# Scaling the exponentials of a banded attention by their inverse sums before they are transposed

## The chip, the cores and the metric

The kernel runs on one core of a Trainium2 chip. The metric is the device time of one execution in microseconds. Three runs of the kernel before took 2136.72, 2136.96 and 2138.09 us, a median of 2136.96 us.

The engines have these names in the profile: PE is TensorE (matrix products and transposes), DVE is VectorE, ACT is ScalarE, POOL is GpSimd, SP issues the DMAs. Each runs its own queue in order, and semaphores join the queues.

## The reference

A banded attention feeds a mixture of experts. Only the attention is touched by the change:

```python
scores = scale * np.matmul(q, k.transpose(0, 1, 3, 2))
...
scores = np.where(keep, scores, -1000000000.0)
scores = scores - np.max(scores, axis=-1, keepdims=True)
a = np.exp(scores)
a = a / (np.sum(a, axis=-1, keepdims=True) + 1e-09)
return np.matmul(a, v).astype(np.float32)
```

The sizes are 4 batches, 8 heads, 768 positions and a head width of 64. A query sees the first 8 keys and the 96 keys that end with itself. All is float32. Behind it, 3072 rows of width 512 go through a gate, eight Sinkhorn steps on the gate's weights, and 8 experts with a hidden width of 1024.

## The kernel before, in words

The attention is cut into 32 pieces of work: batch, half of the sequence, and pair of heads. A piece n has three tiles of 128 queries (UT = 3), and a group is one tile of queries for both heads of the pair, so there are 96 groups t = 3n + group. Because the mask is a band, a tile of queries meets at most two blocks of 128 keys, and a group holds two score blocks of 128x256 (128x128 at the very start of a sequence). Groups are handled in chunks of two (CHUNK = 2), so the attention stage is 48 chunks.

For one chunk the steps are these, and one chunk's score steps run two chunks ahead of its transposes (AHEAD = 4 groups):

- `prepare` (L251 on): TensorE transposes the queries and keys of a later piece; ScalarE copies the result rounded (L266), VectorE subtracts to get the remainder (L267), and GpSimd copies key blocks (L275 to L282). The next load of q and k is issued behind it.
- `scores`: TensorE multiplies into two PSUM banks, one for each head of the pair, both groups side by side. There is only one buffer for each bank, so the next chunk's products wait until VectorE has read this one's.
- `softmax` (L335, L339): VectorE adds the bias, writes the block to `p_sb` in SBUF and gets the row's extreme in `mx`; ScalarE takes the exponential in place and sums each row into `sm`.
- After the last group of a piece (L342 to L345) VectorE adds EPS to the six columns of `sm` and takes the reciprocal; ScalarE spreads the result over 64 columns for each head, into `inv`, 128x384.
- `turn`: TensorE transposes the exponentials, ScalarE copies them to `pT`.
- `place`, `flush`: when the piece ends, `invert` has TensorE transpose `inv` (three 128x128 blocks, `r_ps`) and VectorE copy it back (L450). TensorE multiplies the transposed exponentials with the values into `o_ps`. VectorE multiplies `o_ps` by `inv` (L436), ScalarE copies it rounded to `xh` (L439), and VectorE subtracts to get `xl` (L441). `flush` also issues the load of the values of piece n + 2.

So the outputs come out transposed, the queries along the columns, and the inverse sums have to be turned and spread before they can be multiplied with them.

Beside the attention, in the same stage and in the gaps that `between` gives it, run parts of the expert layer: hidden layers of the first expert on TensorE, the gate, and sums of the attention's outputs (`combine`, L684 to L694) on GpSimd, 128x512 each. DMAs are issued by SP alone.

TensorE's order in the attention is that of the program. The other engines' orders are set by a scheduler when the kernel is built.

Of the kernel before, what the change touches and what calls it, by code (L numbers as in the profile page):

```python
# [8 lines left out]
F32 = mybir.dt.float32  # L9
# [3 lines left out]
ALU = mybir.AluOpType  # L13
# [4 lines left out]
P = 128  # L18
# [4 lines left out]
EPS = 1e-9  # L23
UT = 3
# [23 lines left out]
GROUPS = (((0, 0), (1, 0)), ((0, 1), (1, 1)), ((0, 2), (1, 2)))  # L48
# [44 lines left out]
class InOrder:  # L93


    def __init__(self, tc):
        self.tc, self.engine = tc, tc.nc.tensor
# [8 lines left out]
class Banded:  # L106
# [6 lines left out]
    def __init__(self, tc, q, k, v, early):  # L113

        self.tc, self.nc = tc, tc.nc
        self.q, self.k, self.v = q, k, v
        self.H, self.D = q.shape[1], q.shape[3]
        H, nb = self.H, 3 * self.H * P
        self.bias1 = early[:, 0:2 * H * P].rearrange("p (h c) -> p h c", h=H)
        self.bias0 = early[:, 2 * H * P:nb].rearrange("p (h c) -> p h c", h=H)  # L120
        self.early_raw = early[:, nb:nb + self.RAW]
        nb += self.RAW
        self.d1 = early[:, nb:nb + 2 * P]
        self.d0 = early[:, nb + 2 * P:nb + 3 * P]
        self.work = [(b, half, g) for b in range(q.shape[0]) for half in range(2) for g in range(H // 2)]
        self.pending = []
        self.sums, self.inv, self.outs = {}, {}, {}
        self.pe = InOrder(tc)
        nb += 3 * P
        self.early_pT = early[:, nb:nb + 4 * P].rearrange("p (c k) -> p c k", c=4)  # L130
        assert nb + 4 * P <= early.shape[1] - 256
        self.warm = early[:, -256:].bitcast(mybir.dt.bfloat16)
        self.qk, self.vs, self.ready, self.scored, self.far, self.copied, self.loaded = {}, {}, {}, {}, {}, {}, {}
# [182 lines left out]
    def softmax(self, t, s_list):  # L316


        nc, D = self.nc, self.D
        n, group = divmod(t, len(GROUPS))  # L320
        _, half, g = self.work[n]
        blocks = self.key_blocks(half)[1]
        p_sb = self.wrk.tile([P, 2, 2, P], F32, name="p_sb")
        mx = self.wrk.tile([P, 2], F32, name="mx", bufs=4)
        if group == 0:
            self.sums[n] = self.wrk.tile([P, UT, 2], F32, name="sm", bufs=4)
        sm = self.sums[n]
        views = []
        for u, (j, i) in enumerate(GROUPS[group]):
            h = 2 * g + j  # L330
            nb = len(blocks[i])
            bias = self.bias0[:, h] if nb == 1 else self.bias1[:, h]
            pv = p_sb[:, u, 0:nb].rearrange("p a c -> p (a c)")
            views.append(pv)
            nc.vector.tensor_tensor_reduce(out=pv, in0=s_list[u], in1=bias, scale=-(D ** -0.5), scalar=3.0e38,  # L335
                                           op0=ALU.add, op1=ALU.min, accum_out=mx[:, u:u + 1])
        for u, pv in enumerate(views):
            j, i = GROUPS[group][u]
            nc.scalar.activation(out=pv, in_=pv, func=AF.Exp, bias=mx[:, u:u + 1], scale=-1.0,  # L339
                                 accum_out=sm[:, i, j:j + 1])  # L340
        if group == len(GROUPS) - 1:
            nc.vector.tensor_scalar(out=sm, in0=sm, scalar1=EPS, scalar2=None, op0=ALU.add)  # L342
            nc.vector.reciprocal(out=sm, in_=sm)
            self.inv[n] = self.wrk.tile([P, UT, P], F32, name="inv", bufs=3)
            nc.scalar.copy(out=self.inv[n].rearrange("p t (j d) -> p (t j) d", j=2),  # L345
                           in_=sm.rearrange("p t j -> p (t j)").unsqueeze(2).broadcast_to([P, 2 * UT, D]))
        return p_sb

    def blocks(self, n, group):
# [63 lines left out]
    def place(self, turned, x):  # L413

        for t, pT in turned:
            n, group = divmod(t, len(GROUPS))
            if group == len(GROUPS) - 1:
                self.invert(n)
            if group == 0:
                self.outs[n] = self.ps.tile([P, UT, P], F32, name="o_ps", tag="o", bufs=2)  # L420
            self.pending.append((n, group, pT, self.outs[n], n % (self.H // 2), x))

    def flush(self):


        ended = None
        for n, group, pT, o_ps, g, x in self.pending:
            self.values(n, group, pT, o_ps)
            if group == len(GROUPS) - 1:
                ended = n, o_ps, g, x  # L430
        self.pending = []
        if ended is None:
            return
        n, o_ps, g, x = ended
        self.load_v(n + 2)
        self.nc.vector.tensor_tensor(out=o_ps, in0=o_ps, in1=self.inv.pop(n), op=ALU.mult)  # L436
        of = o_ps.rearrange("p t c -> p (t c)")
        for xh, xl, src, dst, width in x:
            self.nc.scalar.copy(out=xh[:, g, dst:dst + width], in_=of[:, src:src + width])  # L439
        for xh, xl, src, dst, width in x:  # L440
            self.nc.vector.tensor_tensor(out=xl[:, g, dst:dst + width], in0=of[:, src:src + width],  # L441
                                         in1=xh[:, g, dst:dst + width], op=ALU.subtract)

    def invert(self, n):

        inv = self.inv[n]
        r_ps = self.ps.tile([P, 4, P], F32, name="r_ps", tag="tp") if self.idle else self.turned("r_ps")
        for i in range(UT):
            self.pe.transpose(out=r_ps[:, i], in_=inv[:, i], identity=self.ident)
        self.nc.vector.tensor_copy(inv, r_ps[:, 0:UT])  # L450


class Dense:
# [938 lines left out]
```

## Time and profile before

The profiled execution took 2136.92 us, and its span from the first to the last instruction is 2135.1 us.

| what | before |
|---|---|
| median of three runs | 2136.96 us |
| profiled execution | 2136.92 us |
| its span | 2135.1 us |
| mean granted TensorE clock | 0.999 |
| first and last start of the score operation (L335) | 12.2 and 262.6 us |
| last start of L441, the remainder of an output | 276.7 us |
| TensorE busy, 400 to 1000 us | 600.0 of 600 us |

The attention stage is about the first 277 us. What follows is the expert layer. A row of groups gives the line, the engine, the operation, output and inputs by their names in the program, the shapes and the count; then the busy time in us and the mean of one instruction in ns; then the time that the engine sat idle just ahead of it, with what ended it. A row of a line's or a tile's instructions gives the shortest, the median and the longest in ns, and the first and last start in us. A row of the timeline gives the start and the duration in us.

### The profile page before, as it was taken

How to read it: one execution, taken by the hardware profiler on the slowest of the kernel's cores; microseconds unless marked ns; L12 is line 12 of the kernel's file. 1: busy time of each engine (PE TensorE's matmuls, PEld its weight loads, DVE VectorE, ACT ScalarE, POOL GpSimd, SP SyncE). 2: the span in 40 equal slices, each digit the busy share in tenths (PEclk: the TensorE clock that was granted, in tenths of full speed). 3: DMA queues.
4: the chain of work that ended last, by engine and by line, in shares of the span. 5: the costliest groups of instructions: out<-in, count | busy, mean ns of one | idle time of the engine just before them, and what ended most of it. 6: DMA issues, size and time to landing. Idle time of an engine off the chain costs nothing.

```text
span 2135.1 us, 31170 instructions
## 1 busy us (share of the span) xinstructions
PE 2107.4 (99%) x10440; PEld 1729.6 (81%) x10441; DVE 1492.1 (70%) x2278; ACT 744.8 (35%) x1539; POOL 1513.6 (71%) x1361
## 2 busy tenths in 40 slices
PE   9999999999999999999999999999999999999998
PEld 6877768888888888888888888888788888888886
DVE  7666678655555565557777777777667777777776
ACT  7778743333332333323222222222242222222221
POOL 5685887777777777537777777777767777777775
PEclk9999999999999999999999999999999999999999
DMA  6687555756657566597777777777976777677662
GB/s 157 156 215 184 141 201 218 266 220 244 232 212 265 210 234 238 203 395 224 202 195 204 203 195 203 203 196 202 340 242 194 203 203 199 199 203 203 194 194 82
DMA packets 294872, 452.40 MB, mean 212 GB/s; under 512 B 114160, under 2 KB 153264, under 8 KB 284336
## 3 DMA queue, kind: packets, MB, share of 16 engines
q1 hardware_dynamic: 294704, 450.31, 67.5%
q8 instruction: 87, 1.43, 0.3%
q14 instruction: 81, 0.66, 0.1%
HBM read 310.92 MB, written 139.30 MB: 211 GB/s over the span
## 4 chain that ended last, share of the span: by engine, by line
PE 94%; DVE 3%; ACT 2%; POOL 1%; issue 0%; DMA 0%; SPq 0%; DVEq 0%; POOLq 0%; ACTq 0%
PE m_ps L100 27%; PE y_ps L100 16%; PE bank_x L100 11%; PE bank_z L100 11%; PE bank_w L100 11%; PE bank_y L100 6%; PE s_ps L100 2%; PE o_ps L100 2%; PE t_ps L103 1%; PE h_ps L100 1%; ACT p_sb L339 1%; PE tp L103 1%; PE y_ps L774 1%; PE y_ps L775 1%; PE y_ps L776 1%; DVE sm L342 0%
## 5 line engine op out<-in xcount | busy, mean ns | idle before, releaser
L100 PE MATMUL m_ps<-hop,w2r 128*128 128x512 f32 x2520 | 639.5, 389 | 1.4 <-DVE m L1298 1.4
L1298 DVE TENSOR_TENSOR m<-m_ps,m 128x1024 f32<-128x1024 f32 x406 | 495.3, 1220 | 194.6 <-PE m_ps L100 191.4
L100 PEld LDWEIGHTS m_ps<-hop,w2r 128*128 128x128 f32 x2520 | 472.9, 188 | 100.2 <-DVE m L1298 1.8
L872 POOL TENSOR_TENSOR hop<-h,hop 128x512 fp32r<-128x512 f32 x180 | 233.1, 1295 | 303.4 <-ACT hop L871 303.4
L100 PE MATMUL y_ps<-w2ops,hop 128*128 128x512 f32 x1344 | 336.8, 389 | 0.0
L872 POOL TENSOR_TENSOR hop<-hsum,hop 128x512 fp32r<-128x512 f32 x240 | 305.1, 1292 | 0.9 <-ACT hop L871 0.9
L871 ACT CAST hop<-hsum 128x512 fp32r<-128x512 f32 x240 | 149.5, 623 | 426.6 <-POOL hsum L877 423.0
L100 PEld LDWEIGHTS y_ps<-w2ops,hop 128*128 128x128 f32 x1344 | 252.3, 188 | 52.3
L1145 DVE SCALAR_TENSOR_TENSOR acc<-y_ps,pm,acc 128x512 f32<-128x512 f32 x240 | 179.8, 750 | 143.1 <-PE y_ps L100 141.9
L871 ACT CAST hop<-h 128x512 fp32r<-128x512 f32 x180 | 111.8, 621 | 379.2 <-DVE h L883 373.8
L100 PE MATMUL bank_z<-xr,w1r 128*128 128x512 f32 x744 | 189.0, 389 | 0.0
L100 PE MATMUL bank_w<-xr,w1r 128*128 128x512 f32 x744 | 189.0, 389 | 0.0
L100 PE MATMUL bank_x<-xr,w1r 128*128 128x512 f32 x744 | 188.9, 389 | 0.0
L877 POOL TENSOR_TENSOR hsum<-h,h 128x512 f32<-128x512 f32 x120 | 153.1, 1297 | 41.1 <-DVE h L883 41.0
L100 PEld LDWEIGHTS bank_x<-xr,w1r 128*128 128x128 f32 x744 | 139.6, 188 | 28.9
L100 PEld LDWEIGHTS bank_z<-xr,w1r 128*128 128x128 f32 x744 | 139.5, 188 | 28.8
L100 PEld LDWEIGHTS bank_w<-xr,w1r 128*128 128x128 f32 x744 | 139.5, 188 | 28.8
L877 POOL TENSOR_TENSOR hsum<-h,hsum 128x512 f32<-128x512 f32 x120 | 155.4, 1295 | 0.0
L339 ACT ACTIVATE p_sb<-p_sb,mx 128x256 f32<-128x256 f32 (+1 forms) x192 | 93.0, 493 | 34.9 <-DVE mx L335 34.9
L615 POOL TENSOR_TENSOR wsum<-w1f 128x256 f32<-128x256 f32 x62 | 44.9, 746 | 84.7 <-DMA w1f<-in_moe_w_dram 84.7
L100 PE MATMUL bank_y<-xr,w1r 128*128 128x512 f32 x372 | 94.4, 389 | 0.0
L748 DVE TENSOR_TENSOR t<-bank_y,t 128x512 f32<-128x512 f32 x93 | 64.2, 690 | 39.2 <-PE bank_y L100 38.2
(263 smaller groups left out, 3383.9 us busy)
## 6 DMA issues: line engine op xcount, KB each, us to landing
w1r<-w1s SPq DMA_DIRECT2D x434, 256.0 KB, 3.0
w2r<-w2s SPq DMA_DIRECT2D x420, 256.0 KB, 3.0
w1s<-w1ops SPq DMA_DIRECT2D x31, 1792.0 KB, 6.8
w2s<-s2ops SPq DMA_DIRECT2D x30, 1024.0 KB, 8.4
w2s<-w2ops SPq DMA_DIRECT2D x30, 768.0 KB, 7.7
w1f<-in_moe_w_dram SPq DMA_DIRECT2D x32, 512.0 KB, 7.8
w2f<-in_moe_w_dram SPq DMA_DIRECT2D x32, 512.0 KB, 8.6
xs_t<-piece SPq DMA_DIRECT2D x16, 512.0 KB, 3.5
```

The costliest lines, as they stand in the source:

```text
L100: return self.tc.keep_in_program_order(self.engine.matmul(*args, **kw))
L103: return self.tc.keep_in_program_order(self.engine.transpose(*args, **kw))
L339: nc.scalar.activation(out=pv, in_=pv, func=AF.Exp, bias=mx[:, u:u + 1], scale=-1.0, accum_out=sm[:, i, j:j + 1])
L615: self.nc.gpsimd.tensor_tensor(out=s[:, n], in0=x, in1=y, op=op)
L748: tt(out=t, in0=bank["y"], in1=t, op=ALU.add)
L774: self.pe.matmul(y_ps, lhsT=hh, rhs=lf, start=(f == 0), stop=False, skip_group_check=True)
L775: self.pe.matmul(y_ps, lhsT=hl, rhs=wf, start=False, stop=False, skip_group_check=True)
L871: self.nc.scalar.copy(out=t[:, 0], in_=full)
L872: self.nc.gpsimd.tensor_tensor(out=t[:, 1], in0=full, in1=t[:, 0], op=ALU.subtract)
L877: self.nc.gpsimd.tensor_tensor(out=t, in0=self.full[x], in1=self.full[y], op=ALU.subtract)
L1145: nc.vector.scalar_tensor_tensor(out=a, in0=y_ps, scalar=moe.pm[:, tt, e:e + 1], in1=a, op0=ALU.mult, op1=ALU.add)
L1298: nc.vector.tensor_tensor(out=ms[p], in0=bank, in1=ms[p], op=ALU.add)
```

## The change

Each group's sums are made ready on their own, the exponentials are multiplied with the inverse sums in SBUF, ahead of their transposes, and everything that turned and applied the inverse sums later is taken out.

```diff
-        if group == 0:
-            self.sums[n] = self.wrk.tile([P, UT, 2], F32, name="sm", bufs=4)
-        sm = self.sums[n]
+        sm = self.wrk.tile([P, 2], F32, name="sm", bufs=4)
...
         for u, pv in enumerate(views):
-            j, i = GROUPS[group][u]
             nc.scalar.activation(out=pv, in_=pv, func=AF.Exp, bias=mx[:, u:u + 1], scale=-1.0,
-                                 accum_out=sm[:, i, j:j + 1])
-        if group == len(GROUPS) - 1:
-            nc.vector.tensor_scalar(out=sm, in0=sm, scalar1=EPS, scalar2=None, op0=ALU.add)
-            nc.vector.reciprocal(out=sm, in_=sm)
-            self.inv[n] = self.wrk.tile([P, UT, P], F32, name="inv", bufs=3)
-            nc.scalar.copy(out=self.inv[n].rearrange("p t (j d) -> p (t j) d", j=2),
-                           in_=sm.rearrange("p t j -> p (t j)").unsqueeze(2).broadcast_to([P, 2 * UT, D]))
+                                 accum_out=sm[:, u:u + 1])
+        nc.vector.tensor_scalar(out=sm, in0=sm, scalar1=EPS, scalar2=None, op0=ALU.add)
+        nc.vector.reciprocal(out=sm, in_=sm)
+        for u, pv in enumerate(views):
+            nc.vector.tensor_scalar(out=pv, in0=pv, scalar1=sm[:, u:u + 1], scalar2=None, op0=ALU.mult)
         return p_sb
...
-            if group == len(GROUPS) - 1:
-                self.invert(n)
...
-        self.nc.vector.tensor_tensor(out=o_ps, in0=o_ps, in1=self.inv.pop(n), op=ALU.mult)
...
-    def invert(self, n):
-
-        inv = self.inv[n]
-        r_ps = self.ps.tile([P, 4, P], F32, name="r_ps", tag="tp") if self.idle else self.turned("r_ps")
-        for i in range(UT):
-            self.pe.transpose(out=r_ps[:, i], in_=inv[:, i], identity=self.ident)
-        self.nc.vector.tensor_copy(inv, r_ps[:, 0:UT])
```

Where the scheduler puts the new instructions is seen in VectorE's queue. Before, this stands between the score operations of the 29th and the 30th chunk (the number behind a score buffer tells the buffers apart; ISA is the score operation, L335):

```order
L342 TENSOR_SCALAR sm<-sm 128x6
L343 RECIPROCAL sm<-sm 128x6
L267 TENSOR_TENSOR qq<-tp,qq 128x384
L436 TENSOR_TENSOR o_ps<-o_ps,inv 128x384
L267 TENSOR_TENSOR kk<-tp,kk 128x3x128
L441 TENSOR_TENSOR xl<-o_ps,xh 128x384
L335 ISA p_sb,mx<-s_ps_2861,acc 128x256
```

Now, at the same place, where the line numbers are those of the changed kernel (L338 was L342, L333 was L335, L433 was L441, and L341 is the new multiplication):

```order
L338 TENSOR_SCALAR sm<-sm 128x2
L339 RECIPROCAL sm<-sm 128x2
L338 TENSOR_SCALAR sm<-sm 128x2
L341 TENSOR_SCALAR p_sb<-p_sb,sm 128x256 x2
L339 RECIPROCAL sm<-sm 128x2
L267 TENSOR_TENSOR qq<-tp,qq 128x384
L267 TENSOR_TENSOR kk<-tp,kk 128x3x128
L341 TENSOR_SCALAR p_sb<-p_sb,sm 128x128 x2
L433 TENSOR_TENSOR xl<-o_ps,xh 128x384
L333 ISA p_sb,mx<-s_ps_2947,acc 128x256
```

The product with the outputs is gone, and both groups of the chunk now have their addition, their reciprocal and their two multiplications between one chunk's score operations and the next one's; the remainders of q and k stand behind the first group's multiplications.

On TensorE, this stood just ahead of the next chunk's score products before:

```order
L100 MATMUL o_ps<-acc 64x128 x2
L100 MATMUL o_ps<-pT,acc 64x128 x4
L103 MATMUL t_ps<-ident,p_sb 128x128 x6
L103 MATMUL r_ps<-ident,inv 128x128 x3
L100 MATMUL s_ps_2936<-kk,qq 128x256
```

Now the same place reads:

```order
L100 MATMUL o_ps<-acc 64x128 x2
L100 MATMUL o_ps<-pT,acc 64x128 x4
L103 MATMUL t_ps<-ident,p_sb 128x128 x6
L100 MATMUL s_ps_3023<-kk,qq 128x256
```

The three transposes of the inverse sums are gone, and nothing else of TensorE's order has moved there.

More of the change, by code (lines that the diff above doesn't have):

```diff
@@ L126, in __init__ @@
         self.pending = []
-        self.sums, self.inv, self.outs = {}, {}, {}
+        self.outs = {}
         self.pe = InOrder(tc)
```

## The prediction

> **What bounds the kernel now.** The page's first part and the shares of the chain that ended last come first.
>
> ```profile
> PE 2107.4 (99%) x10440; PEld 1729.6 (81%) x10441; DVE 1492.1 (70%) x2278; ACT 744.8 (35%) x1539; POOL 1513.6 (71%) x1361
> ...
> PE 94%; DVE 3%; ACT 2%; POOL 1%; issue 0%; DMA 0%; SPq 0%; DVEq 0%; POOLq 0%; ACTq 0%
> ```
>
> TensorE is busy 99% of the span and holds 94% of the chain, so taking work from TensorE should pay and giving work to VectorE (70%) should not matter. Those are averages over the whole span. The change touches the attention stage alone, so the table by windows comes next, cut at 277 us, where the last attention output is split.
>
> ```profile
> core 0: us, PE busy (x) PEld busy (x) DVE busy (x) ACT busy (x) POOL busy (x), PEclk, DMA share, GB/s
> 0.00:277.00 277.00, 263.67 (x2290) 206.21 (x2291) 184.26 (x661) 213.12 (x658) 189.75 (x263) 1.00 0.65 168
> ```
>
> In this stage TensorE is busy for 263.7 of 277 us at the full granted clock. VectorE has 184 us of work and GpSimd 190 us, so VectorE has some 90 us to give, and GpSimd runs beside it 69% of the time. The beat of the stage is read from the score operation, which runs once per chunk of two groups for each of four score blocks:
>
> ```profile
> L335 DVE CUSTOM_DVE_ANT_0 p_sb<-s_ps,acc x192: 285/420/428, 12.2 to 262.6; 128x256 f32<-128x256 f32 x160, 128x128 f32<-128x128 f32 x32
> ```
>
> 192 of them are 48 chunks. Their starts spread over 250.4 us, so **a chunk takes 250.4 / 47 = 5.33 us**, and TensorE sets it. The question is whether VectorE can still keep that beat.
>
> **What goes.** These groups, all of the stage, disappear or shrink:
>
> ```profile
> L103 PE MATMUL r_ps<-ident,inv 128*128 128x128 f32 x96 | 15.8, 274 | 0.9 <-ACT acc L361 0.9
> ...
> L436 DVE TENSOR_TENSOR o_ps<-o_ps,inv 128x384 f32<-128x384 f32 x32 | 18.0, 562 | 21.9 <-PE o_ps L100 21.6
> L342 DVE TENSOR_SCALAR sm<-sm 128x6 f32<-128x6 f32 x32 | 17.9, 560 | 27.9 <-ACT p_sb L339 27.9
> L450 DVE COPY inv<-r_ps 128x384 f32<-128x384 f32 x32 | 17.7, 553 | 8.2 <-PE r_ps L103 7.8
> ```
>
> The 96 transposes occupied TensorE for 15.8 us (they overlap, so it is not 96 times 274 ns). That is **the most that the change can win**: 15.8 / 48 = 0.33 us a chunk, which would leave TensorE a beat of 5.0 us. VectorE is rid of 18.0 + 17.7 us, and ScalarE of a copy that is off the path.
>
> **What comes.** Per chunk VectorE gets two additions of EPS (two columns wide), two reciprocals and four multiplications of a block of exponentials, in all 96, 96 and 192 where there were 32, 32 and none. The rows for the parts:
>
> ```profile
> L175 DVE TENSOR_SCALAR acc<-acc x4: 280/282/545, 10.1 to 10.9; 128x256 f32<-128x256 f32 x4
> ...
> L342 DVE TENSOR_SCALAR sm<-sm x32: 160/542/1367, 20.5 to 264.2; 128x6 f32<-128x6 f32 x32
> L343 DVE RECIPROCAL sm<-sm x32: 181/192/193, 21.1 to 264.4; 128x6 f32<-128x6 f32 x32
> ```
>
> The multiplication has no row. Its nearest relative is the same operation on the same shape in L175: 0.28 us when nothing disturbs it. All four of those fit into this row,
>
> ```profile
> 10.07 1.16 DVE L175 TENSOR_SCALAR acc<-acc 128x256 f32<-128x256 f32 x4
> ```
>
> so without the one long call (545, or 0.26 over the others) they follow each other at (1.16 - 0.26 - 0.28) / 3 = 0.2 us. A pair costs 0.48.
>
> Far more telling is the addition on six columns: 160 ns at best, 1367 at worst, and 17.9 us / 32 = 560 ns on average. Two of them beside GpSimd's work show why:
>
> ```profile
> 153.78 0.42 DVE L335 CUSTOM_DVE_ANT_0 p_sb<-s_ps,acc 128x256 f32<-128x256 f32 x1 [0.23 <-PE s_ps L100]
> ...
> 155.76 0.80 DVE L342 TENSOR_SCALAR sm<-sm 128x6 f32<-128x6 f32 x1 [0.78 <-ACT p_sb L339]
> 156.60 0.19 DVE L343 RECIPROCAL sm<-sm 128x6 f32<-128x6 f32 x1
> ...
> 161.78 1.27 DVE L342 TENSOR_SCALAR sm<-sm 128x6 f32<-128x6 f32 x1 [1.11 <-ACT p_sb L339]
> ```
>
> ```profile
> 155.26 1.28 POOL L693 TENSOR_TENSOR xsum<-xsum,xres 128x512 f32<-128x512 f32 x1
> ...
> 161.75 1.26 POOL L691 TENSOR_TENSOR xsum<-xh 128x512 f32<-128x512 f32 x1
> ```
>
> Both additions end within 0.04 us of the end of the GpSimd operation beside them (156.56 against 156.54, 163.05 against 163.01). **This operation stands still until GpSimd's is over**, while the reciprocal is never stretched (193 at most). The average loss is 560 - 160 = 400 ns. The new multiplications are the same operation, SBUF to SBUF.
>
> The Trainium skill (SBUF — State Buffer, "Who interferes with whom") states it as a rule against this change: a `tensor_scalar` may run in a mode with two ports and then shares a pair of ports with GpSimd, and whichever started first keeps the pair for its whole instruction. The trace agrees, with the two ends above. By that rule the multiplications wait as the additions do; without it they would cost their own length alone, and the result would be that of the first rival below.
>
> **The sum, by chunk.** VectorE works in order. From the first score operation to the moment when a group's sums are there it is 155.76 - 153.78 = 1.98 us; ScalarE's exponentials set that and the change leaves them alone. Then per group 0.16 (addition) + 0.19 (reciprocal) + 0.48 (two multiplications) + 0.08 (two steps of 0.04 between dependent operations, as from 156.56 to 156.60) = 0.91, twice. What is left of VectorE's work stands between them:
>
> ```profile
> L267 DVE TENSOR_TENSOR kk<-tp,kk 128x384 fp32r<-128x384 f32 x32 | 17.6, 549 | 2.5 <-ACT kk L266 2.5
> L267 DVE TENSOR_TENSOR qq<-tp,qq 128x384 fp32r<-128x384 f32 x32 | 17.3, 540 | 1.7 <-ACT qq L266 1.6
> ...
> L441 DVE TENSOR_TENSOR xl<-o_ps,xh 128x384 fp32r<-128x384 f32 x24 | 13.3, 555 | 4.5 <-ACT xh L439 3.8
> ...
> L715 DVE SCALAR_TENSOR_TENSOR fhop<-h_ps,fhop 128x512 fp32r<-128x512 f32 x6 | 4.1, 688 | 2.8 <-ACT fhop L714 2.8
> L441 DVE TENSOR_TENSOR xl<-o_ps,xh 128x256 fp32r<-128x256 f32 x8 | 3.4, 420 | 1.0 <-ACT xh L439 0.8
> L441 DVE TENSOR_TENSOR xl<-o_ps,xh 128x128 fp32r<-128x128 f32 x8 | 2.3, 285 | 1.0 <-ACT xh L439 1.0
> ```
>
> They are 58.0 us, or 1.21 a chunk. Together 1.98 + 1.82 + 1.21 = **5.0 us without any wait for GpSimd**. That alone is TensorE's new beat; there is no room left. The waits come on top.
>
> A chunk has six operations that can be stopped. Bounds: none is stopped (0), or every microsecond of GpSimd's 190 stops VectorE (4.0 a chunk). The nearest row is the addition's 0.40. I charge it five times, not six, because the second multiplication of a pair starts before the first has ended, and of L175's four only one was caught. GpSimd's work does not grow, so with a longer chunk it fills a smaller part: the wait is 0.40 x 5.33 / C for a chunk of C. Then C = 5.0 + 5 x 0.40 x 5.33 / C, which gives C = 6.6. The stage grows by 47 x (6.63 - 5.33) = **61 us**. What is queued behind the stopped operations is all that VectorE does for TensorE: the next chunk's score operations, which free the two score banks, and the lower halves of q and k. So TensorE waits, and the delay reaches the end. The expert stage behind it keeps its work and its order.
>
> The profiled execution took 2136.92 us (span 2135.1 and 1.8 around it), within 0.04 of the median of the runs. 2136.9 + 61 = **2198 us**.
>
> Costed at nothing: the copy of the inverse on ScalarE (off the path), the first chunk's longer way to its transposes (about 1 us once), and GpSimd's own waits for the multiplications, as it had 87 us idle in the stage.
>
> **Rivals.**
> First, TensorE stays the bound and the kernel is faster. The place is VectorE's queue in each chunk: if the multiplications are not stopped, or fall where GpSimd stands still, C stays at 5.0 and the stage wins up to 15.8 us: 2121. Against it stands 0.40 us on 32 additions, for it only that GpSimd is light early on (busy for 28.4 of 63 us, against 153.1 of 202 later):
>
> ```profile
> 12.00:75.00 63.00, 28.43 (x60) 1.00 0.68 164
> 75.00:277.00 202.00, 153.11 (x181) 1.00 0.64 174
> ```
>
> It decides at C = 5.33, a total wait of 0.3 us a chunk, less than one average addition's. Chance 0.14, and 0.06 that it just breaks even.
>
> Second, light waits: half the price (0.20) gives C = 5.9 and +28, 2165. From 2141 to 2165: 0.12.
>
> Third, GpSimd and VectorE take turns: whenever VectorE releases the ports, the waiting GpSimd operation goes first, and each multiplication meets a whole one of 1.28. All six at 0.40 with no thinning give 5.0 + 2.4 = 7.4 and +98, 2235; the outer bound of 4.0 a chunk gives 9.0 and +171, 2308. Above 2240: 0.06.
>
> **How the numbers follow.** The forecast, 2165 to 2240, has 0.62. The range 2133 to 2240 leaves out the faster case (0.14) and the heaviest (0.06). 0.2% is about what a measurement of this kernel can tell from no change (4.3 us): faster 0.14, the same 0.06, slower 0.80.
>
> **What would show it.** The multiplications should average well over 0.28 us, with ends at the ends of GpSimd's operations. VectorE's busy time up to the last attention output should come near the stage's length, TensorE's share there should fall to some 75%, and its longest waits should be for VectorE's maxima, qq and kk. Score operations should spread over some 310 us. If the multiplications take 0.28 flat, the lock is the wrong step. If they are long but the spread stays near 250 us, VectorE had more room than the walk gives it. If the stage grows and the end does not, the expert stage gave it back.

## The result, and the profile after

The changed kernel took 2190.93 us, the median of 6 runs (2189.5 to 2195.35), against 2136.84 us for the kernel before in the same comparison: 1.0254 times as long (95% interval 1.0244 to 1.0265), 54 us more. The forecast was 2198 us.

The first part of the changed kernel's page and the shares of the chain that ended last:

```profile
PE 2125.0 (97%) x10345; PEld 1737.5 (79%) x10345; DVE 1576.6 (72%) x2534; ACT 735.0 (34%) x1507; POOL 1516.4 (69%) x1361
...
PE 88%; DVE 8%; ACT 2%; issue 1%; DMA 0%; POOL 0%; SPq 0%; DVEq 0%; POOLq 0%; ACTq 0%
```

VectorE's share of the whole span rose by two points only, yet its share of the chain went from 3% to 8%. The attention stage shows it. TensorE's last product with the values now ends at 332.6 us, against 275.6 us before. The stage's row, up to 332 us:

```profile
0.00:332.00 332.00, 278.63 (x2183) 213.24 (x2185) 266.65 (x916) 201.42 (x624) 192.32 (x263) 0.92 0.53 139
```

VectorE has 267 us of recorded work where it had 184. In the other 65 us it mostly waits: 28.7 us for ScalarE's sums, 10.5 for ScalarE's copies of the outputs, and 10.2 for scores (counted up to 340 us). TensorE, busy for 95% of the stage before, is busy for 84% of a longer one, at a mean granted clock of 0.92, where it had 1.00. GpSimd's work is the same (192 us, 263 operations, against 190 and 263). The score operation and the new operations, one row a line of the program:

```profile
L333 DVE CUSTOM_DVE_ANT_0 p_sb<-s_ps,acc x192: 276/415/426, 12.2 to 316.1; 128x256 f32<-128x256 f32 x160, 128x128 f32<-128x128 f32 x32
...
L341 DVE TENSOR_SCALAR p_sb<-p_sb,sm x192: 271/350/2449, 14.9 to 321.3; 128x256 f32<-128x256 f32 x160, 128x128 f32<-128x128 f32 x32
L338 DVE TENSOR_SCALAR sm<-sm x96: 149/170/1230, 14.4 to 319.9; 128x2 f32<-128x2 f32 x96
L339 DVE RECIPROCAL sm<-sm x96: 144/165/167, 14.6 to 320.1; 128x2 f32<-128x2 f32 x96
```

The score operations spread over 303.9 us instead of 250.4: 6.47 us a chunk instead of 5.33. The profiled execution took 2195.35 us, 58.4 more than the one before. 53.5 of them are in this spread, 3.5 between the last score operation and the last product with the values, and 1.4 behind that. Multiplications and additions have medians of 350 and 170 ns and worst cases of 2449 and 1230, while the reciprocal never exceeds 167. Some of these operations of one chunk, VectorE's timeline first (the two multiplications one by one), GpSimd's behind it:

```profile
169.53 0.66 DVE L338 TENSOR_SCALAR sm<-sm 128x2 f32<-128x2 f32 x1 [0.62 <-ACT p_sb L336]
...
170.43 1.24 DVE L341 TENSOR_SCALAR p_sb<-p_sb,sm 128x256 f32<-128x256 f32 x1
171.59 1.35 DVE L341 TENSOR_SCALAR p_sb<-p_sb,sm 128x256 f32<-128x256 f32 x1
...
172.86 1.22 DVE L338 TENSOR_SCALAR sm<-sm 128x2 f32<-128x2 f32 x1
```

```profile
168.89 1.27 POOL L677 TENSOR_TENSOR xsum<-xsum,xres 128x512 f32<-128x512 f32 x1
170.24 1.27 POOL L678 TENSOR_TENSOR piece<-xsum,piece 128x512 fp32r<-128x512 f32 x1
171.48 1.31 POOL L668 TENSOR_TENSOR xres<-xl 128x512 f32<-128x512 f32 x1
172.75 1.30 POOL L675 TENSOR_TENSOR xsum<-xh 128x512 f32<-128x512 f32 x1
```

With the reciprocal between them, these VectorE operations need about 1.1 us and take 4.6. The first addition ends with L677 (170.19 against 170.16), the first multiplication 0.16 us behind L678 (171.67 against 171.51), the second 0.15 us behind L668 (172.94 against 172.79), and the second addition with L675 (174.08 against 174.05). It is so through the whole stage: by the trace, 60 of the 61 multiplications that are longer than 0.45 us end less than 0.2 us behind the end of a GpSimd operation, and all 35 additions longer than 0.25 us end within 0.1 us of one. Behind these operations stand the remainders of q, for which TensorE then waits. TensorE's waits in the stage, longest first in total:

```profile
PE s_ps L100 <- DVE qq L267: 27.5, 14, 3.6
PE t_ps L103 <- DVE p_sb L341: 5.4, 5, 2.6
PE s_ps L100 <- DVE kk L267: 5.2, 6, 3.0
```

### The profile page after: what moved, and what is told of

It is laid out like the page before. It is cut to its first block, busy times and chain, and to the rows that moved or that the text cites. A ratio compares the mean times of both kernels' runs of the same rounds, so it can differ in the third digit from the quotient of the medians.

```text
span 2193.5 us, 31192 instructions
## 1 busy us (share of the span) xinstructions
PE 2125.0 (97%) x10345; PEld 1737.5 (79%) x10345; DVE 1576.6 (72%) x2534; ACT 735.0 (34%) x1507; POOL 1516.4 (69%) x1361
## 4 chain that ended last, share of the span: by engine, by line
PE 88%; DVE 8%; ACT 2%; issue 1%; DMA 0%; POOL 0%; SPq 0%; DVEq 0%; POOLq 0%; ACTq 0%
PE m_ps L100 26%; PE y_ps L100 16%; PE bank_w L100 11%; PE bank_z L100 11%; PE bank_x L100 11%; PE bank_y L100 5%; DVE p_sb L341 3%; ACT p_sb L336 2%; PE s_ps L100 1%; DVE sm L338 1%; PE o_ps L100 1%; PE t_ps L103 1%; PE h_ps L100 1%; PE tp L103 1%; DVE p_sb L333 1%
## 5 line engine op out<-in xcount | busy, mean ns | idle before, releaser
L341 DVE TENSOR_SCALAR p_sb<-p_sb,sm 128x256 f32<-128x256 f32 (+1 forms) x192 | 100.0, 564 | 1.6
```

The costliest lines, as they stand in the source:

```text
L341: nc.vector.tensor_scalar(out=pv, in0=pv, scalar1=sm[:, u:u + 1], scalar2=None, op0=ALU.mult)
```

## The experiments

Three theories stood against each other: waits (VectorE's additions and multiplications stand still behind GpSimd), length (what is new on VectorE is simply too long), and clock (TensorE at a lower granted clock is what costs). Ratios are to the kernel before, in the same comparison. One thing limits the runs that edit VectorE's own operations: the scheduler then builds VectorE's queue anew, and some operations change places within a chunk. With the summing form, 22 of the first 42 chunks have the order of the changed kernel. The run with GpSimd's sums left out has it in all 42.

**GpSimd's sums left out, in the changed kernel and in the kernel before.** The same edit in both:

```diff
-            moe.right_sums(part, new, xtmp, b == NB - 1 and h == 1)
+            if b == NB - 1:
+                moe.right_sums(part, new, xtmp, h == 1)
...
-                moe.fetch(t, x_spill[b][o])
+                moe.fetch(t, x_spill[b][o if o[0] == "b" else "b11"])
```

The spills of the sums are dropped with them.

> The changed kernel without GpSimd's sums of the attention's outputs for the first two thirds of the rows (these operands and their spills to DRAM are left out; the expert stage loads another stored operand of the same size in their place). VectorE's and TensorE's attention work is untouched. Waits theory (VectorE's additions and multiplications stand still behind GpSimd): the waits of some 80 us in the stage mostly go, the chunk falls from 6.44 us to 5.0 to 5.3, the time to 2120 to 2140 us, and the multiplications average under 0.36 us. Length theory (the new operations' own length and their chain fill VectorE's queue, the waits are absorbed): 2180 us or more. Clock theory (TensorE, granted 0.86 to 0.93 in parts of the stage, is what is slow): 2180 us or more, with the clock still low.

> The control: the kernel before with the same work left out of GpSimd. All theories: GpSimd is not on the path there, so 2125 to 2140 us. If this fell as far as the changed kernel does, the gain of the other run would not be VectorE's waits.

Measured: 2142.58 us for the changed kernel (1.0031, 1.0020 to 1.0043) and 2131.85 us for the kernel before (0.9974, 0.9965 to 0.9984). Without this GpSimd work, 48 us of the changed kernel's time go, and 5 us of the other's. The loss shrinks from 54 us to 11. The same groups of operations in the changed kernel, as it is and then without the sums (busy us, mean ns of one):

```profile
L341 DVE TENSOR_SCALAR p_sb<-p_sb,sm 128x256 f32<-128x256 f32 x160 | 90.5, 608 | 1.4
L338 DVE TENSOR_SCALAR sm<-sm 128x2 f32<-128x2 f32 x96 | 38.0, 398 | 29.1 <-ACT p_sb L336 28.7
```

```profile
L341 DVE TENSOR_SCALAR p_sb<-p_sb,sm 128x256 f32<-128x256 f32 x160 | 64.3, 445 | 1.4
L338 DVE TENSOR_SCALAR sm<-sm 128x2 f32<-128x2 f32 x96 | 20.2, 213 | 28.4 <-ACT p_sb L336 27.9
```

Two groups of instructions whose code and order were not touched lost a quarter to a half of their length when another engine was relieved. The mean of 445 is above the 0.36 us expected and the time 3 us above the range. GpSimd still has work there that stops VectorE: of the 31 multiplications longer than 0.45 us, 14 end with its key copies, and most others with the sums that are left or its work on the first expert's weights.

**Multiplications of 2 columns.**

```diff
-            nc.vector.tensor_scalar(out=pv, in0=pv, scalar1=sm[:, u:u + 1], scalar2=None, op0=ALU.mult)
+            nc.vector.tensor_scalar(out=pv[:, 0:2], in0=pv[:, 0:2], scalar1=sm[:, u:u + 1], scalar2=None, op0=ALU.mult)
```

> The changed kernel with each multiplication cut to 2 of its 256 (or 128) columns, so most exponentials stay unscaled; number, place and kind of the instructions stay. Waits theory: each still stands behind GpSimd's operation, only its own 0.1 us or so goes: 2160 to 2185 us, and the mean of the 2-column multiplications is 0.35 us or more against 0.16 alone. Length theory: VectorE's own work falls under TensorE's beat, 2120 to 2135 us.

Measured: 2164.06 us (1.0124, 1.0108 to 1.0141).

```profile
L341 DVE TENSOR_SCALAR p_sb<-p_sb,sm x192: 210/224/2347, 14.8 to 296.4; 128x2 f32<-128x2 f32 x192
```

An operation on two columns still takes up to 2347 ns, and 418 ns on average, above the 350 that the waits theory asked for. With 99% of the multiplications' data gone, half of the loss (27 us) is left. With the other half went 0.13 us of length each (350 to 224), four times a chunk, so length counts too. The waits shrank as well (the additions from 398 to 329 ns on average), and the run does not part the two.

**No addition of EPS**, then **the multiplication in a form that also sums**, then both together.

```diff
-        nc.vector.tensor_scalar(out=sm, in0=sm, scalar1=EPS, scalar2=None, op0=ALU.add)
         nc.vector.reciprocal(out=sm, in_=sm)
```

```diff
-            nc.vector.tensor_scalar(out=pv, in0=pv, scalar1=sm[:, u:u + 1], scalar2=None, op0=ALU.mult)
+            nc.vector.tensor_scalar(out=pv, in0=pv, scalar1=sm[:, u:u + 1], scalar2=0.0, op0=ALU.mult, op1=ALU.add,
+                                    accum_out=junk[:, u:u + 1])
```

The tile `junk` holds the sums, which nothing reads.

> The changed kernel without the addition of EPS to the sums (each sum holds the exponential of its own maximum, which is 1, and 1 + 1e-9 is 1 in float32). Two of the six operations of a chunk that can be stopped go, with 24 us of waits and 0.2 us each of length and step. Waits theory: 0.9 us a chunk, less what later operations wait instead: chunk 5.7 to 6.0, 2150 to 2170 us. Length theory: 0.4 us a chunk, 19 us, 2172 us.

> The changed kernel with each multiplication in the form that also writes out a sum of its results (which nothing reads): the same data, one result a cycle, so longer, about 0.42 to 0.5 us for 256 columns against 0.35. Waits theory, if this form does not share GpSimd's ports: it is never stretched (longest under 0.6 us), the chunk is longer by itself by 0.6 to 0.7 us and shorter by the multiplications' waits of 0.9 us: chunk 6.1 to 6.4, 2170 to 2190 us, no slower than the changed kernel's 2191. Length theory: 0.6 us a chunk more, 2215 to 2225 us.

> The same, and without the addition of EPS (it changes no sum, see above): no operation of the change can be stopped by GpSimd any more. Waits theory: chunk 5.3 to 5.6, 2135 to 2155 us, far below the kernel without the addition alone (2176), although its multiplications are longer. Length theory: longer multiplications than in that kernel, so 2185 us or more.

| kernel | us | ratio (95% interval) |
|---|---|---|
| changed | 2190.93 | 1.0254 (1.0244 to 1.0265) |
| changed, no addition | 2176.37 | 1.0186 (1.0169 to 1.0203) |
| changed, summing form | 2159.84 | 1.0100 (1.0083 to 1.0117) |
| changed, both | 2140.86 | 1.0015 (1.0005 to 1.0024) |

The multiplication's row in the kernel without the addition, in the one with the summing form, and in the one with both:

```profile
L340 DVE TENSOR_SCALAR p_sb<-p_sb,sm x192: 268/353/2435, 14.6 to 304.8; 128x256 f32<-128x256 f32 x160, 128x128 f32<-128x128 f32 x32
```

```profile
L342 DVE TENSOR_SCALAR_CACHE_REDUCE p_sb<-p_sb,sm x192: 329/475/481, 14.9 to 292.7; 128x256 f32<-128x256 f32 x160, 128x128 f32<-128x128 f32 x32
```

```profile
L341 DVE TENSOR_SCALAR_CACHE_REDUCE p_sb<-p_sb,sm x192: 335/475/481, 14.6 to 268.9; 128x256 f32<-128x256 f32 x160, 128x128 f32<-128x128 f32 x32
```

This is the sharpest test. The summing form is longer by itself, 475 ns against 350, and it is never stretched: 481 at most. The kernel becomes 31 us faster with an instruction that is a third longer, and below the 2170 to 2190 us expected. With no new operation left that GpSimd can stop, 50 of the 54 us are gone. The length theory wanted 2185 us or more there, and falls as an account of its own. No run parts the form from the changed places in the queue, but none of the 192 multiplications is stretched, whatever its place.

The addition alone gave 15 us, outside the waits theory's range and close to the 19 us of the length theory. The waits did not go with it, they moved: the wide multiplications average 680 ns there, where they had 608. Once the multiplications could not be stopped, taking the addition out gave 19 us.

**Products that keep TensorE busy.** The prediction says nothing of the granted clock. In the changed kernel it moved, to 0.86 in the window from 175 to 200 us. It drops at 176.0 us, to 0.50 as the row shows. TensorE's timeline there stands behind a wait of 3.40 us:

```profile
176.00:179.00 3.00, 3.00 (x9) 2.22 (x8) 2.32 (x16) 1.86 (x8) 0.00 (x0) 0.50 0.00 0
```

```profile
174.78 0.95 PE L100 MATMUL s_ps<-kk,qq 64*128 64x128 f32 x11 [3.40 <-DVE qq L267]
...
176.83 0.63 PE L100 MATMUL g_ps<-xh,ghl 128*128 128x512 f32 x1
177.25 0.63 PE L100 MATMUL g_ps<-xl,ghl 128*128 128x512 f32 x1
```

The products then start 0.42 us apart; at a clock of 1.00 those of this shape start 0.23 us apart (333.10 and 333.33 us). The edit:

```diff
+            if t + AHEAD < len(self.work) * len(GROUPS):
+                self.keep_warm(*self.fill, 4)
             self.ahead(range(t + AHEAD, t + AHEAD + CHUNK))
```

> The changed kernel with four bf16 products of 128x512 on TensorE ahead of each chunk's score products, about 0.9 us at full clock, into a PSUM tile that nothing reads. The changed kernel's trace shows a dozen stretches at a granted clock of 0.5 in the stage, behind waits of TensorE of some 3 us. Clock theory (a part of the loss is TensorE at half clock, on the path): the granted clock returns to 0.97 or more in the stage and the time falls to 2170 to 2185 us. Waits theory alone: the clock returns too, the time stays at 2188 to 2200 us, as the products fill time that TensorE waited or lengthen the chunks that TensorE sets.

Measured: 2192.4 us (1.0252, 1.0234 to 1.0269), no change. In the stage (up to 332 us) the clock came back from 0.92 to 0.96, short of the 0.97 that both theories expected, and TensorE had 298.7 us of recorded work instead of 278.6. That the time did not move speaks against the clock as a main cause. It does not exclude a few us, which the added products may have taken back.

**Multiplications left out, and also without the addition.**

```diff
-        for u, pv in enumerate(views):
-            nc.vector.tensor_scalar(out=pv, in0=pv, scalar1=sm[:, u:u + 1], scalar2=None, op0=ALU.mult)
```

> The changed kernel without the multiplications (the outputs stay unscaled): sums, additions and reciprocals stay, the transposes of the inverse sums are gone. Both theories: TensorE's beat of 5.0 us returns, 2119 to 2127 us; this is the gain that was on TensorE.

> The changed kernel without multiplications and without the addition of EPS (outputs stay unscaled): what TensorE wins by the 96 transposes when nothing new on VectorE can be stopped. If the gain of 15.8 us was there and the additions took the rest of it in the run without multiplications (2132.5): 2119 to 2127 us. If TensorE's own beat is not 5.0 us: 2128 to 2133 us.

Measured: 2132.51 us (0.9972, 0.9960 to 0.9985), and 2127.28 us without the addition (0.9951, 0.9938 to 0.9965). The first missed its range: the additions, 96 where there were 32, take 5 us of the gain. They last 170 ns at the median there, 463 on average and up to 2186. The second sits at the upper edge of its range, 2127: 9.5 us less than before, with nothing new on VectorE that can be stopped. That is not all TensorE's, as the last run below shows.

**Versions meant to beat both.** One multiplication of each group on ScalarE, the other on VectorE in the summing form or in the short one, both without the addition; and the kernel before without the addition.

```diff
-            nc.vector.tensor_scalar(out=pv, in0=pv, scalar1=sm[:, u:u + 1], scalar2=None, op0=ALU.mult)
+            if u:
+                nc.scalar.activation(out=pv, in_=pv, func=AF.Copy, scale=sm[:, u:u + 1])
+            else:
+                nc.vector.tensor_scalar(out=pv, in0=pv, scalar1=sm[:, u:u + 1], scalar2=0.0, op0=ALU.mult, op1=ALU.add,
+                                        accum_out=junk)
```

> A try for a version that beats both: no addition of EPS, one multiplication of each group on ScalarE (a copy scaled per row), the other on VectorE in the form that is never stretched. VectorE's chain by the rows measured so far is 1.98 + 2 x 0.72 + 1.21 = 4.6 us a chunk, under TensorE's beat: 2122 to 2135 us by the waits theory. If ScalarE (253 us recorded in the stage, 48 more here) sets the time instead, 2140 to 2160 us.

> The same with VectorE's multiplication in the short form that GpSimd can stop, twice a chunk. Waits theory: 0.1 to 0.2 us shorter each by itself, 0.3 us of wait each: as fast as or up to 8 us slower than the version never stretched, 2125 to 2143 us. Length theory: faster than that version by 0.25 us a chunk, where VectorE sets the time.

> The kernel before without the addition of EPS (32 instructions, 18 us of VectorE's time, 13 of them waits). Waits theory: VectorE was not what set the time there, so 2132 to 2137 us, 0 to 5 us less.

Measured: 2139.76 us with the summing form (1.0011, 1.0002 to 1.0020), 2142.63 us with the short one (1.0027, 1.0017 to 1.0037), and 2132.50 us for the kernel before without the addition (0.9979, 0.9969 to 0.9989). Neither beats the kernel before. The first missed the 2122 to 2135 us hoped for and came to the edge of the range for ScalarE setting the time; the second stayed within its range, at the slow end. Taking half of the multiplications from VectorE is not told apart from leaving them all there in the summing form (1.0011 against 1.0015, and the intervals overlap). In the version with the summing form, TensorE's largest wait in the stage comes to 4.5 us in total, for the remainders of k. No single wait carries it; what sets the time there was not settled. The kernel before without its 32 additions is faster than both kernels, by 0.2% (4 us) against the kernel before: the addition changes no value (each sum holds the exponential of its own maximum, 1, and 1 + 1e-9 is 1 in float32), and it was stopped by GpSimd there too. Beside it, the run without multiplications and additions wins 2132.50 - 2127.28 = 5.2 us by what the change takes out.

## Why the prediction was right, step by step

- **TensorE's gain (15.8 us).** Mis-sized. The run without multiplications and additions shows 9.5 us at best, and 4.2 of these come from the additions of the kernel before alone. About 5 us are left for the transposes, the product with the outputs and the copies. A chunk takes (254.8 - 12.2) / 47 = 5.16 us in that run, not 5.0. Why the 15.8 us of TensorE's busy time do not come out in full was not traced.
- **The multiplication's own length (0.28 us, a pair 0.48).** Mis-sized. Undisturbed it takes 0.35, and a pair 0.62, as in the row below. That is 0.28 us a chunk more than the sum had. The relative in L175 multiplies by a constant, this one by a column; that this is the reason was not isolated. The reciprocal is 0.165 instead of 0.19.

```profile
178.66 0.62 DVE L341 TENSOR_SCALAR p_sb<-p_sb,sm 128x256 f32<-128x256 f32 x2
```

- **The wait for GpSimd.** The mechanism is shown, by the runs with GpSimd's sums left out, by the form that is not stopped, and by the ends that fall together. The price, 5 x 0.32 = 1.6 us a chunk, came out at about 1.4: 96 x (398 - 150) ns of additions and 160 x (608 - 350) of wide multiplications are 65 us, over 48 chunks. The ground for charging five instead of six was wrong. The second of a pair is not spared: it lasts 0.58 us on average over the stage, the first 0.55, and at 171.59 us it stood behind a GpSimd operation that had started at 171.48. All six wait, so the price of one is 1.4 / 6 = 0.23 us, less than the 0.32 charged and than the additions before had suggested.
- **The sum.** That C = 6.6 met 6.47 is in part luck. A length too short by 0.23 us a chunk and a wait too long by 0.2 made up for each other, and so, within the wait, did a count too low (five for six) and a price too high. Put together from the measured terms it is 5.0 + 0.23 + 1.4 = 6.6 as well, 0.1 to 0.2 us more than measured; which step of the walk counts too much was not traced.
- **Who waits.** As forecast: TensorE for the remainders of q and k, which stand in VectorE's queue behind the stopped operations (27.5 and 5.2 us). Its waits for the maxima are small (3.1 us). It waits 5.4 us for the multiplications ahead of the transposes, five times up to 53 us, where the prediction had put about 1 us once.
- **The expert stage** kept its time: of the profiled execution's 58.4 us more, 1.4 lie behind the last product with the values.
- **Rivals.** The first, TensorE as the bound, needed multiplications that are not stopped. With both edits, where nothing new is stopped, VectorE still does not keep TensorE's beat: a chunk is 254.0 / 47 = 5.40 us (score operations from 12.2 to 266.2 us, the row below), though with the longer form of the multiplication. The short form wholly without stops was not run. The second rival's price (0.20, which is 0.18 at its chunk of 5.9) is below the measured 0.23, and it too counted five waits and a length too short. The third was right in that GpSimd goes between the two of a pair, and too dear at 0.40 each.

```profile
L333 DVE CUSTOM_DVE_ANT_0 p_sb<-s_ps,acc x192: 285/419/426, 12.2 to 266.2; 128x256 f32<-128x256 f32 x160, 128x128 f32<-128x128 f32 x32
```

- **Signs.** The wide multiplications average 0.61 us, and the score operations spread over 303.9 us (310 foretold). TensorE's share was foretold at some 75% and is 84%; part of it is work at half clock, which is recorded as busy. VectorE's busy time did not come near the stage's length: it is 267 of 332 us, and the rest is mostly the waits named above.

## What to carry to other kernels

Before work is given to an engine with idle time, look at the spread of its instructions' lengths beside the other engine's timeline: an operation whose worst case is eight times its best, and that ends where another engine's ends, can bring that wait with it, and each instruction that is added is one more that can be stopped. A longer form of the same instruction that is not stopped may be the faster one. And on a queue that is nearly full, count every instruction by itself, for here the short ones waited as long as the wide: 398 - 150 ns on average for an addition on two columns, 608 - 350 for a wide multiplication.

## What was not expected of the hardware

- With GpSimd's next operation ready, VectorE's two multiplications in a row did not run together: the first ended with one GpSimd operation, the second with the next (2.51 us for a pair of 0.62).
- The multiplication that also writes a sum took 475 ns at the median and 481 at most on the same data, beside the same GpSimd work that stretched the plain form to 2449.
- The multiplication by a column took 0.35 us where a multiplication by a constant took 0.28 (L175; both 128x256, SBUF to SBUF, float32). On two columns it took 224 ns, where the addition of a constant took 170. Other differences between these operations were not excluded.
- In the changed kernel the granted clock fell to 0.86 in some windows of 25 us, behind waits of TensorE; before it stood at 1.00 through the whole stage. The Trainium skill (TensorE: Matmul & The Clock Gate, "Part 1: The HAM clock gate (the "warmup" mystery)") gives an idle window of about 3.4 us for the drop to half rate. The trace agrees on the half rate, with 0.50 from 176.0 us on and the products 0.42 us apart. It differs on the wait: there were 3.40 us of waiting ahead of that drop, but only 1.42 ahead of the one at 275.0 us, in the row below.

```profile
273.74 0.50 PE L100 MATMUL s_ps<-kk,qq 64*128 64x256 f32 x4 [1.42 <-DVE qq L267]
```
